# Expert 0's rows by one-hot products instead of a gather, three experts' lists from one-hot rows, and weight loads held back

## The chip, the cores and the metric

The kernel runs on one core of one Trainium2 chip. The metric is the device time of one execution in microseconds (us); smaller is better. Beside it stands a profile of one execution: what each engine did, when it waited and for whom. The engines are TensorE (PE, matrix products), VectorE (DVE), ScalarE (ACT), GpSimd (POOL) and SyncE (SP, which issues DMA transfers).

## What is computed

```
x   = attention(q, k, v)           # 2 x 8 heads, 768 positions, 64 wide; only where both hash to one bucket
x   = (silu(x @ w_in)) @ w_out     # 1536 tokens, 512 -> 2048 -> 512
do  = x @ w_skip > 0               # tokens that go on
e   = argmax(x[do] @ w_gate)       # one of 8 experts; gate = its softmax weight
y   = gate * (relu(x[do] @ w1[e]) @ w2[e])     # 512 -> 1024 -> 512
out = x;  out[do] = x[do] + y
```

## The kernel before

The work has three stages: attention, the MLP, and the experts. All is fp32; the large products are made of two halves each, a rounded high half (whi, xTh, gh) and the rest as low half (wlo, xTl, gl), three products for one. The high half is a copy on ScalarE, the low half a subtraction on VectorE.

**MLP.** The 1536 tokens go in three blocks of 512 (four tiles of 128 tokens each), the 16 pieces of the weights inside. When a block is done, its rows go to a DRAM buffer `x_d` and to the output, and for the first two blocks the gate logits are made on VectorE (`logit`, four per piece of the next block). Then `route` turns the logits of a block into places: which expert each token goes to, and its rank there, by small products with a triangular matrix. The tokens' numbers go to a list in DRAM, `id_d`, by an indirect DMA per tile (`tk` by `slot`), and the running lists of experts 0 and 1 are also made on chip: `oh` is a one-hot row per token, and `idx` and `idx1` are small products of it with the tokens' numbers.

**The bridge.** The third block is computed turned (features by tokens). It is turned back (`xt`), stored, and routed in the same way, expert 0 first, so that its rows can be gathered from `x_d` by an indirect DMA (`fetch_x(0)`) as soon as their list is there; then expert 1, the places of all tokens, and the gates (`gates`, `gp`, `gT`, `g_d`). Filler products (`em_busy`) stand between PE's steps.

**Experts.** `plan` is a list of steps, written out by hand, that sets the order: `("h", e, c, j)` is half a hidden block of expert e (12 products for a block, 6 in a step, `eh`), `t` turns it (`tr`, then hT0h/hT0l or hT1h/hT1l), `y` is the second product (`ey`), `x` turns the gathered rows of an expert (xTh/xTl), and after its last `y` an expert's result `eo` is scattered to the output. The weights of an expert are 8 pieces of 512 KB, 64 in all. Raw pieces land in 20 buffers (12 in `ring`, 8 in `more`; `fill` loads the next). `splitting` makes the two halves of a piece in one of 7 homes, and `ahead`, after most steps of the plan, splits as many further pieces as there are free homes. So in each engine's queue the halves of a piece stand up to seven pieces ahead of its use. Each engine works through its queue in order.

`fill(n, True)` loads n pieces, each behind a tiny memset on POOL, so that they start only when POOL has come to that place in its queue; `cnt["hold"]` stops all other loads.

## Time and profile before

| | |
|---|---|
| median of three runs | 622.31 us (621.67 to 625.53) |
| the profiled execution's own time | 622.04 us |
| its span, first to last instruction | 620.3 us |
| mean granted TensorE clock | 0.998 of full speed |
| busy: PE, DVE, ACT, POOL | 97%, 75%, 65%, 27% of the span |
| last MLP product ends, expert 0 begins (PE) | 499.13 us, 511.72 us |

Busy shares are means over three stages with different limits. A busy PE is not a PE at its peak. What a change in one stage is worth must be read from that stage: which wait ends last there.

### The profile page before, as it was taken

To read this page: it belongs to the slowest core of one execution; us is meant where nothing else is said; L and a number is where in the kernel's file an instruction comes from. 1 tells how busy PE (TensorE), PEld (TensorE's weight loads), DVE (VectorE), ACT (ScalarE), POOL (GpSimd) and SP (SyncE) were. 2 spreads that over 40 slices of the span, in tenths; PEclk is the share of its full clock that TensorE was granted. 3 is DMA by queue.
4 is the path that set the end of the run, shared out by engine and by line. 5 is a ranking of instruction groups with operands and counts; after the bars stand their busy time and mean duration, and the time that the engine had idled before them with its cause. 6 is when DMAs were issued, how large, how long until landed. Compare 5 with 4: busy or idle time off the path is not lost.

```text
span 620.3 us, 9579 instructions
## 1 busy us (share of the span) xinstructions
PE 604.2 (97%) x3263; PEld 463.3 (75%) x3263; DVE 465.7 (75%) x861; ACT 400.7 (65%) x671; POOL 167.3 (27%) x256
## 2 busy tenths in 40 slices
PE   8899999999999999999999999999999979999996
PEld 5767667676666757788888887788888857788885
DVE  6877777888787667799747775457885469899992
ACT  6988888888877985466554333443334456888881
POOL 5535637373653143000000000020000054534101
PEclk9999999999999999999999999999999999999999
DMA  4433542524324131666423000024232349999900
GB/s 134 144 113 93 174 124 58 157 66 137 79 66 122 46 115 52 214 216 229 143 89 121 1 1 1 1 47 164 97 103 101 118 150 257 395 408 408 391 20 28
DMA packets 30978, 83.47 MB, mean 135 GB/s; under 512 B 6032, under 2 KB 9810, under 8 KB 30798
## 3 DMA queue, kind: packets, MB, share of 16 engines
q1 hardware_dynamic: 28834, 79.06, 38.6%
q0 software_dynamic: 1936, 3.65, 1.7%
q8 instruction: 26, 0.43, 0.3%
q14 instruction: 26, 0.21, 0.1%
q10 hardware_dynamic: 156, 0.11, 0.1%
HBM read 67.66 MB, written 8.50 MB: 123 GB/s over the span
## 4 chain that ended last, share of the span: by engine, by line
PE 87%; DVE 4%; ACT 3%; DMA 2%; issue 2%; POOL 1%; SPq 0%; POOLq 0%; DVEq 0%; ACTq 0%
PE ph L605 20%; PE o L648 13%; PE S L385 11%; PE T L411 10%; PE pv L425 10%; PE o L639 7%; PE eh L1046 6%; PE ey L1068 6%; ACT P L399 1%; PE tr L1024 1%; PE pj L337 1%; DVE wlo L252 1%; PE bs L472 1%; DMA w<-in_mw_dram 1%; ACT K L317 1%
## 5 line engine op out<-in xcount | busy, mean ns | idle before, releaser
L252 DVE TENSOR_TENSOR wlo<-wraw,whi 128x1024 fp32r<-128x1024 f32 x100 | 119.6, 1222 | 5.8 <-ACT whi L249 4.9
L249 ACT CAST whi<-wraw 128x1024 fp32r<-128x1024 f32 x100 | 102.7, 1050 | 20.0 <-DVE wraw L223 13.1
L399 ACT ACTIVATE P<-S,bs 128x768 f32<-128x768 f32 x96 | 95.5, 994 | 27.1 <-DVE bs L397 25.3
L611 ACT ACTIVATE g<-ph 128x512 f32<-128x512 f32 x48 | 28.6, 597 | 119.8 <-PE ph L605 113.1
L395 DVE TENSOR_REDUCE mx<-S 128x1 f32<-128x768 f32 x96 | 91.1, 949 | 11.1 <-PE S L385 8.8
L385 PE MATMUL S<-K,Q 88*128 88x384 f32 (+1 forms) x384 | 92.3, 361 | 3.1 <-ACT P L399 3.0
L411 PEld LDWEIGHTS T<-ident,P 128*128 128x128 f32 x576 | 68.1, 141 | 30.8 <-ACT PT L414 22.1
L411 PE MATMUL T<-ident,P 128*128 128x128 f32 x576 | 88.7, 277 | 0.2 <-ACT PT L414 0.2
L613 DVE TENSOR_TENSOR gl<-g,gh 128x512 fp32r<-128x512 f32 x48 | 33.6, 701 | 68.9 <-ACT gh L612 68.9
L777 POOL DMA_INDIRECT id_d<-tk,slot x12 | 12.2, 1014 | 248.1 <-DVE pre L785 245.0
L425 PE MATMUL pv<-PT,v 128*64 128x384 f32 x384 | 72.3, 498 | 0.0
L385 PEld LDWEIGHTS S<-K,Q 88*128 88x128 f32 (+1 forms) x384 | 62.7, 191 | 11.7 <-ACT P L399 5.8
L416 DVE COPY PT<-T 128x384 f32<-128x384 f32 x85 | 47.0, 553 | 22.5 <-PE T L411 22.4
L414 ACT COPY PT<-T 128x384 f32<-128x384 f32 x107 | 50.5, 479 | 7.1 <-PE T L411 6.8
L605 PE MATMUL ph<-xhi,whi 128*128 128x512 f32 x192 | 52.9, 397 | 0.0
L605 PE MATMUL ph<-xhi,wlo 128*128 128x512 f32 x192 | 51.8, 392 | 0.7 <-DVE wlo L252 0.7
L605 PE MATMUL ph<-xlo,whi 128*128 128x512 f32 x192 | 51.9, 392 | 0.0
L325 POOL TENSOR_TENSOR K<-raw,K 64x192 fp32r<-64x192 f32 x56 | 31.6, 594 | 53.9 <-ACT K L317 28.9
L661 DVE CUSTOM_DVE_ANT_0 junk<-x,gwb 128x512 bf16<-128x512 f32 x72 | 45.4, 687 | 0.0
L330 POOL TENSOR_TENSOR Q<-raw,Q 64x192 fp32r<-64x192 f32 x64 | 36.1, 592 | 28.1 <-ACT Q L320 26.4
L605 PEld LDWEIGHTS ph<-xhi,wlo 128*128 128x128 f32 x192 | 36.0, 188 | 9.0 <-DVE wlo L252 1.2
L425 PEld LDWEIGHTS pv<-PT,v 128*64 128x64 f32 x384 | 23.4, 136 | 25.7 <-issue 25.6
(173 smaller groups left out, 1045.6 us busy)
## 6 DMA issues: line engine op xcount, KB each, us to landing
wraw<-in_w_dram SPq DMA_DIRECT2D x64, 512.0 KB
w<-in_mw_dram SPq DMA_DIRECT2D x32, 512.0 KB
v<-in_vt_dram SPq DMA_DIRECT2D x8, 384.0 KB
rb<-r_d SPq DMA_DIRECT2D x32, 96.0 KB
out_dram<-x SPq DMA_DIRECT2D x12, 256.0 KB
x_d<-x SPq DMA_DIRECT2D x11, 256.0 KB
raw<-in_kT_dram SPq DMA_DIRECT2D x7, 384.0 KB
raw<-in_qT_dram SPq DMA_DIRECT2D x7, 384.0 KB
```

What stands on the lines that cost most here:

```text
L249: nc.scalar.copy(hi[:, sl], t[:, sl])
L252: eng.tensor_tensor(lo[:, sl], t[:, sl], hi[:, sl].bitcast(F32), op=ALU.subtract)
L385: nc.tensor.matmul(ps[:, c, 0:HQ], q_[0:n, hd, q0:q0 + P], k_[0:n, hd, c * HQ:(c + 1) * HQ], start=first, stop=not first)
L395: nc.vector.tensor_reduce(mx[:, 0:1], ps[:, :, 0:HQ], axis=AX.XY, op=ALU.max, negate=True)
L399: nc.scalar.activation(pt.rearrange("p (a b) -> p a b", a=2), ps[:, :, 0:HQ], AF.Exp, bias=bs_[:, 0:1], scale=bs_[:, 1:2], accum_out=st_su ...
L411: nc.tensor.transpose(ps[:, j], pt[:, k * P:(k + 1) * P], ident)
L414: nc.scalar.copy(dst, ps)
L416: nc.vector.tensor_copy(dst, ps)
L425: nc.tensor.matmul(st_pv[u][hd * D:(hd + 1) * D], vts[i][:, k, hd], st_PT[u][:, hd, k], start=(k == 0), stop=(k == KT - 1))
L605: nc.tensor.matmul(p_[:, 0:c1 - c0], w[:, k * P:(k + 1) * P], x[:, k, t0 * P + c0:t0 * P + c1], start=(q == 0), stop=(q == len(ops3) - 1))
L648: nc.tensor.matmul(acc[t], g[:, (t - t0) * P:(t - t0 + 1) * P], w[:, DM:PIECE], start=(f == 0 and q == 0), stop=(f == NF - 1 and q == 2))
L661: nc.vector.tensor_tensor_reduce(junk, xts[t], pools["gwb_t"][:, c], op0=ALU.mult, op1=ALU.add, scale=1.0, scalar=0.0, accum_out=L[:, t, c ...
```

## The change

Expert 0's rows are no longer gathered before its first product. The rows in the first two blocks are gathered during the MLP's last pieces (`xg0`) and turned (`xT0p`); those in the third block are picked out by fp32 products of its tiles (`late`) with one-hot columns (`ohf`), four for each quarter of the features (`picked`), and the two are added (`summed`) and split (`parted`). The gather `fetch_x(0)` is still made, later, since the result needs the rows themselves. Lists on chip are made for three experts (`NL`), and the DRAM list is read for the other five. Logits of the first blocks come five per piece. In the bridge the logits are made before the tiles are turned, all turned tiles are copied by ScalarE, and there are 5 filler products instead of 37. The low halves of four split pieces, the third list, the places, the gates and their store, the list of the other experts and the largest count now stand between steps of the plan (`between`). Weight loads start behind the gathers of experts 1 and 2, behind that of expert 0, and behind the read of the list, and the last rows' stores to the output behind these; the gates are stored by ScalarE's queue. During expert 0's steps `ahead` is not called.

```diff
+++ after.py
     slot = cp.tile([P, NT], I32, name="slot")
     gat = cp.tile([P, NT], F32, name="gat")
-    list1 = cp.tile([P, 1], F32, name="list1")
+    lists = cp.tile([P, NL], F32, name="lists")
     eid = cp.tile([P, NE], I32, name="eid")
...
-    def gathered(ix, src, cols, tag):
-        xg = pools["e"].tile([P, cols], F32, tag=tag, name=tag, bufs=4)
+    def gathered(ix, src, cols, xg):
+        if isinstance(xg, str):
+            xg = pools["e"].tile([P, cols], F32, tag=xg, name=xg, bufs=4)
         nc.gpsimd.indirect_dma_start(
             out=xg, out_offset=None, in_=src, in_offset=bass.IndirectOffsetOnAxis(ap=ix, axis=0),
-            bounds_check=NTOK, oob_is_err=False)
+            bounds_check=src.shape[0] - 1, oob_is_err=False)
...
-        oh0 = onehot(0, pr0, st0)
-        yield
-        for j in range(n):
-            nc.tensor.matmul(idx, oh0[:, j], c_tok[:, t0 + j], start=False, stop=(last and j == n - 1))
-        if last:
-            with nc.allow_low_precision(reason="integers below 2048, exact"):
-                nc.vector.tensor_reduce(eid[:, 0:1], idx, axis=AX.X, op=ALU.add)
-            fetch_x(0)
...
+    def keyed(pr, st, n):
+        key = sm.tile([P, n], F32, tag="key", name="key")
+        nc.vector.scalar_tensor_tensor(key.unsqueeze(2), pr, 1.0, st, op0=ALU.add, op1=ALU.mult)
+        return key
+
+    def onehot(oh, key, n):
+        nc.vector.tensor_tensor(oh, c_iota.unsqueeze(1).to_broadcast([P, n, P]),
+                                key.unsqueeze(2).to_broadcast([P, n, P]), op=ALU.is_equal)
+
+    def places(e, pr, st, n):
+        key = keyed(pr, st, n)
+        oh = sm.tile([P, 5, P], BF16, tag=f"oh{e}", name="oh", bufs=1)
+        onehot(oh[:, 0:n], key, n)
+        return oh
+
+    def listed(dst, oh, t0, t1):
+
+        for j in range(t1 - t0):
+            nc.tensor.matmul(dst, oh[:, j], c_tok[:, t0 + j], start=(j == 0), stop=(j == t1 - t0 - 1))
+
+    def added(dst, ps, e):
         p1 = sm.tile([P, 1], F32, tag="p1", name="p1")
-        nc.vector.tensor_reduce(p1, idx1, axis=AX.X, op=ALU.add)
-        nc.vector.tensor_tensor(eid[:, 1:2] if last else list1, p1, list1, op=ALU.add)
-        if last:
-            fetch_x(1)
-        yield
-
-        sf = sm.tile([P, n], F32, tag="sf", name="sf")
+        nc.vector.tensor_reduce(p1, ps, axis=AX.X, op=ALU.add)
+        nc.vector.tensor_tensor(dst, p1, lists[:, e:e + 1], op=ALU.add)
...
+    def route(t0, t1, Lx, ps):
+
...
+        yield
+        ranks(pr, st, n, NE)
+        yield
+        sl = sm.tile([P, n, NE], F32, tag="sl", name="sl")
+        nc.vector.tensor_tensor(sl, pr, c_e0.unsqueeze(1).to_broadcast([P, n, NE]), op=ALU.add)
+        ohs = [places(e, pr[:, :, e:e + 1], st[:, :, e:e + 1], n) for e in range(NL)]
+        nc.vector.tensor_tensor(sl, sl, st, op=ALU.mult)
+        yield
+        for e in range(NL):
+            listed(ps[:, 464 + 16 * e:467 + 16 * e], ohs[e], t0, t1)
+        for e in range(NL):
+            added(lists[:, e:e + 1], ps[:, 464 + 16 * e:467 + 16 * e], e)
+        if t0:
+            eidp = sm.tile([P, 1], I32, name="eidp", bufs=1)
+            nc.vector.tensor_scalar(eidp, lists[:, 0:1], float(t1 * P), None, op0=ALU.min)
+            xg0 = gathered(eidp, x_d[0:t1 * P + 1], DM, pools["xo"].tile([P, DM], F32, tag="x", name="xg0", bufs=6))
+        slots(t0, t1, sl)
+        counts(t0, t1)
+        if t0:
+            yield
+            yield
+            yield
+            xtp = ps_tile("xtp", [P, KD, P], "O4")
+            for k in range(KD):
+                nc.tensor.transpose(xtp[:, k], xg0[:, k * P:(k + 1) * P], ident)
+            some.append(pools["xo"].tile([P, DM], F32, tag="x", name="xT0p", bufs=6))
+            nc.scalar.copy(some[0], xtp.rearrange("p k c -> p (k c)"))
...
+                for r in (TILES[-1][0] * P, NTOK):
+                    nc.sync.dma_start(x_d[r:r + 1].rearrange("o (p c) -> (o p) c", p=P), zx)
...
-                for j in range(4):
+                for j in range(5):
...
+        assert cnt["spl"] == NM + 3
+        sp = [splitting(NM + i, apart=True) for i in range(3, 7)]
...
+        ex = sm.tile([P, NT, NE], F32, name="gex", bufs=1)
+        nc.scalar.activation(ex[:, 0, 0:1], lists[:, 0:1], AF.Exp, scale=0.0)
...
-        xps = [ps_tile("xt", [P, KD, P], tag) for tag in ("O0", "O1", "H", "O2", "H")]
-        for k0 in (0, 2):
-            for t in range(t1 - t0):
-                for k in (k0, k0 + 1):
-                    nc.tensor.transpose(xps[4 if t == 0 and k0 else t][:, k], xt[k][:, t * P:(t + 1) * P], ident)
...
+        plc = sm.tile([32 * n, P], F32, name="plc", bufs=1)
+        nc.vector.tensor_copy(plc, plt[0:32 * n])
+
+        xps = [ps_tile("xt", [P, KD, P], tag) for tag in ("O0", "O1", "H", "O2")]
         late = []
...
-                (nc.vector.tensor_copy if t % 2 else nc.scalar.copy)(
-                    x[:, sl].rearrange("p (k c) -> p k c", c=P), xps[4 if k0 else t][:, k0:k1])
-                nc.sync.dma_start(x_d[(t0 + t) * P:(t0 + t + 1) * P, sl], x[:, sl])
+
+        def turned(t):
+            for k in range(KD):
+                nc.tensor.transpose(xps[t][:, k], xt[k][:, t * P:(t + 1) * P], ident)
+            x = ep.tile([P, DM], F32, tag="lx" if t < 2 else "eo", name="x")
+            nc.scalar.copy(x, xps[t].rearrange("p k c -> p (k c)"))
+            nc.sync.dma_start(x_d[(t0 + t) * P:(t0 + t + 1) * P], x)
             late.append(x)
...
-        sp = [splitting(NM + i, apart=True, eng=nc.vector) for i in range(3, 7)]
-        for g in sp:
-            next(g)
...
-        em_busy(5)
-        for j, _ in enumerate(route(t0, t1, pl, ps_tile("pr", [P, 512], "O3"), idx, ps_tile("pr0", [P, 512], "O0"))):
-            em_busy((5, 0, 4, 3, 0, 10)[j])
-            if j == 2:
-                fill(3, True)
-        next(gt, None)
+        turned(0)
+        nc.tensor.transpose(plx[:, P:P + 32 * n], plc, ident[0:32 * n, 0:32 * n])
...
+        turned(1)
+        em_busy(3)
+        ranks(pr0, st0, n, 1)
+        base(pr, t0, n, NE)
+        key = keyed(pr0, st0, n)
+        ohf = pools["xo"].tile([P, DM], F32, tag="x", name="ohf", bufs=6).rearrange("p (t c) -> p t c", c=P)
+        for c in range(0, n, 2):
+            onehot(ohf[:, c:c + 2], key[:, c:c + 2], 2)
+        turned(2)
+        turned(3)
+        xT0 = [ps_tile("xT0", [P, 2, P], tag) for tag in ("H", "O0")]
+
+        def picked(k):
+
+            for t in range(n):
+                nc.tensor.matmul(xT0[k // 2][:, k % 2], late[t][:, k * P:(k + 1) * P], ohf[:, t], start=(t == 0), stop=(t == n - 1))
...
+        def summed(j):
+            nc.vector.tensor_tensor(xs0[:, 2 * j:2 * j + 2], xT0[j], xs0[:, 2 * j:2 * j + 2], op=ALU.add)
+            nc.scalar.copy(xTs0[0][:, 2 * j:2 * j + 2], xs0[:, 2 * j:2 * j + 2])
+
+        def parted(j):
+            hi, lo, x = (x[:, 2 * j:2 * j + 2] for x in (*xTs0, xs0))
+            nc.vector.tensor_tensor(lo, x, hi.bitcast(F32), op=ALU.subtract)
...
+        nc.scalar.copy(ohb[:, 0:n], ohf)
+        next(sp[0])
+        choice(t0, t1, pl, mxl)
         nc.vector.tensor_copy(L[:, t0:t1], pl)
-        gp = ps_tile("gp", [P, 512], "O1")
-        nc.tensor.transpose(gp[0:NT, 0:P], gat, ident)
-        gT = sm.tile([NT, P], F32, name="gT", bufs=1)
-        nc.scalar.copy(gT, gp[0:NT, 0:P])
-        nc.sync.dma_start(g_d[0:NTOK].rearrange("(t p) c -> t (p c)", p=P), gT)
-        fill(3, True)
-        fetch_g(0)
...
-        def fetch_list():
-
-            nc.scalar.dma_start(eidr, id_d.rearrange("(e r) c -> e (r c)", e=NE)[2:NE, 0:P])
+        gt = gates(0, NT)
+        next(gt)
+        st = sel[:, t0:t1]
+        picked(0)
+        picked(1)
+        ranks(pr, st, n, NE)
+        summed(0)
+        next(sp[1])
...
+        ohs = [ohb] + [sm.tile([P, 5, P], BF16, tag=f"oh{e}", name="oh", bufs=1) for e in (1, 2)]
+        onehot(ohs[1][:, 0:n], keys[0], n)
+        picked(2)
+        picked(3)
+        parted(0)
+        onehot(ohs[2][:, 0:n], keys[1], n)
+        for e in (0, 1):
+            listed(ps[:, 464 + 16 * e:467 + 16 * e], ohs[e], t0, t1)
+        summed(1)
+        next(sp[2])
+        next(sp[3])
+        added(eid[:, 1:2], ps[:, 480:483], 1)
+        fetch_x(1)
+        added(eid[:, 0:1], ps[:, 464:467], 0)
+        parted(1)
+        next(sp[0], None)
...
-        xTs[0] = parts(xgs[0], "xT", 2)
-        next(sp[0], None)
-        next(sp[1], None)
-        next(sp[2], None)
-        next(sp[3], None)
-        nc.vector.tensor_copy(mxc, mxf)
+        xTs[0] = tuple(xTs0)
+
+        def third_list():
+
+            ps = psE.tile([P, KD, P], F32, tag="T", name="li", bufs=3)
+            listed(ps[:, 0, 0:3], ohs[2], t0, t1)
+            added(eid[:, 2:3], ps[:, 0, 0:3], 2)
+            fetch_x(2)
+            fill(3, True)
+            nc.vector.tensor_tensor(sl, sl, st, op=ALU.mult)
+            slots(t0, t1, sl)
+            fetch_x(0)
+            fill(3, True)
+            next(sp[1], None)
+            next(gt, None)
+
+        def gates_out():
+
+            gp = psE.tile([P, KD, P], F32, tag="T", name="gp", bufs=3)
+            nc.tensor.transpose(gp[0:NT, 0], gat, ident)
+            gT = sm.tile([NT, P], F32, name="gT", bufs=1)
+            nc.scalar.copy(gT, gp[0:NT, 0])
+            nc.scalar.dma_start(g_d[0:NTOK].rearrange("(t p) c -> t (p c)", p=P), gT)
+            fetch_g(0)
+            fetch_g(1)
+            nc.gpsimd.dma_start(eidr, id_d.rearrange("(e r) c -> e (r c)", e=NE)[NL:NE, 0:P])
+            fill(1, True)
+            for t, x in enumerate(late):
+                nc.sync.dma_start(out[(t0 + t) * P:(t0 + t + 1) * P], x)
+            cnt["hold"] = 0
+
+        def other_lists():
+
+            ps = psE.tile([P, KD, P], F32, tag="T", name="eT", bufs=3)
+            nc.tensor.transpose(ps[:, 0, 0:NE - NL], eidr, ident[0:NE - NL, 0:NE - NL])
+            nc.vector.tensor_copy(eid[:, NL:NE], ps[:, 0, 0:NE - NL])
+            fetch_x(3)
+            fetch_g(2)
+
+        def largest():
+
+            ps = psE.tile([P, KD, P], F32, tag="T", name="pc", bufs=3)
+            nc.tensor.matmul(ps[:, 0, 0:NE], c_one, pre[:, NT], start=True, stop=True)
+            nc.vector.tensor_reduce(mxc, ps[:, 0, 0:NE], axis=AX.X, op=ALU.max)
+
+        def one_ahead():
+
+            next(sp[3], None)
+            split(cnt["spl"])
+
+        between = {("h", 0, 0, 0): third_list, ("h", 0, 0, 1): lambda: next(sp[2], None), ("h", 0, 1, 0): gates_out,
+                   ("t", 0, 0): one_ahead, ("y", 1, 0): other_lists, ("h", 3, 0, 0): lambda: counts(t0, t1), ("y", 3, 0): largest}
...
-        for t, x in enumerate(late):
-            nc.sync.dma_start(out[(t0 + t) * P:(t0 + t + 1) * P], x)
-        fill(1, True)
-        cnt["hold"] = 0
-        fill()
...
-            if (what, e, *at) == ("y", 0, 0):
-                fetch_list()
-            if (what, e, *at) == ("h", 1, 0, 0):
-                ps = psE.tile([P, KD, P], F32, tag="T", name="eT", bufs=3)
-                nc.tensor.transpose(ps[:, 0, 0:NE - 2], eidr, ident[0:NE - 2, 0:NE - 2])
-                nc.vector.tensor_copy(eid[:, 2:NE], ps[:, 0, 0:NE - 2])
-                fetch_x(2)
-                fetch_g(2)
-                fetch_x(3)
-
-            if n + 1 == len(plan) or plan[n + 1][0] not in "tx":
+            between.get((what, e, *at), int)()
+            if (e or (what, *at) == ("t", 1)) and (n + 1 == len(plan) or plan[n + 1][0] not in "tx"):
                 ahead()
```

In VectorE's queue, from the low half of expert 1's rows to that of expert 2's (xTl 128x512 each; wlo is the low half of one weight piece, eid the cast of the other experts' list), there stood:

```order
L1018 TENSOR_TENSOR xTl<-tr,xTh 128x512
L1018 TENSOR_TENSOR hT1l<-tr,hT1h 128x512
L252 TENSOR_TENSOR wlo<-wraw,whi 128x1024
L1123 CAST eid<-eT 128x6
L252 TENSOR_TENSOR wlo<-wraw,whi 128x1024 x3
L1076 SCALAR_TENSOR_TENSOR eo<-ey,gg,xg 128x512
L1018 TENSOR_TENSOR hT0l<-tr,hT0h 128x512
L252 TENSOR_TENSOR wlo<-wraw,whi 128x1024 x4
L1018 TENSOR_TENSOR xTl<-tr,xTh 128x512
```

and now stands, with what is ahead of it since expert 0's first turned half (hT0l):

```order
L1060 TENSOR_TENSOR hT0l<-tr,hT0h 128x512
L253 TENSOR_TENSOR wlo<-wraw,whi 128x1024 x2
L1060 TENSOR_TENSOR xTl<-tr,xTh 128x512
L1060 TENSOR_TENSOR hT1l<-tr,hT1h 128x512
L253 TENSOR_TENSOR wlo<-wraw,whi 128x1024 x7
L1118 SCALAR_TENSOR_TENSOR eo<-ey,gg,xg 128x512
L1060 TENSOR_TENSOR hT0l<-tr,hT0h 128x512
L253 TENSOR_TENSOR wlo<-wraw,whi 128x1024 x4
L1162 CAST eid<-eT 128x5
L253 TENSOR_TENSOR wlo<-wraw,whi 128x1024
L1060 TENSOR_TENSOR xTl<-tr,xTh 128x512
```

Eight low halves stood between the two xTl, twelve do now, and the cast of the list has moved behind eleven of them.

In POOL's queue, from the last expert-list gathers of the bridge on (tk by slot is the scatter of token numbers, gg a gather of gates, the memset a weight load's gate), there stood:

```order
L669 DMA xg<-x_d,eid 128x512
L181 MEMSET wraw 1x1 x3
L669 DMA xg<-x_d,eid 128x512
L777 DMA id_d<-tk,slot 12288x1 x4
L181 MEMSET wraw 1x1 x3
L669 DMA gg<-g_d,eid 128x1 x2
L181 MEMSET wraw 1x1
L669 DMA xg<-x_d,eid 128x512
```

and now stand the gathers of experts 1 and 2, the scatters, the gather of expert 0, and the read of the list behind the gates:

```order
L671 DMA xg<-x_d,eid 128x512 x2
L182 MEMSET wraw 1x1 x3
L739 DMA id_d<-tk,slot 12288x1 x4
L671 DMA xg<-x_d,eid 128x512
L182 MEMSET wraw 1x1 x3
L671 DMA gg<-g_d,eid 128x1 x2
L1152 DMA eidr<-id_d 5x128
L182 MEMSET wraw 1x1
L1049 DMA out_dram<-eo,eid 1536x512
```

The read of the list (eidr), which ScalarE's queue issued, has moved onto POOL, ahead of the memset that lets the weight stream go.

On PE the transposition of the gates (gp) stood ahead of expert 0's first product:

```order
L987 MATMUL gp<-ident,gat 12x128
L1024 MATMUL tr<-ident,xg 128x128 x4
L1046 MATMUL eh<-whi,xTh 128x512
L1046 MATMUL eh<-wlo,xTh 128x512
L1046 MATMUL eh<-whi,xTh 128x512
```

and now stands inside expert 0, between its third block of six products and the turning of its first hidden block (hr):

```order
L1088 MATMUL eh<-whi,xTl 128x512 x2
L1146 MATMUL gp<-ident,gat 12x128
L1066 MATMUL tr<-ident,hr 128x128 x4
L1088 MATMUL eh<-whi,xTh 128x512
L1088 MATMUL eh<-wlo,xTh 128x512
```

The turning of the gathered rows (tr from xg) ahead of expert 0 is gone, and gp has moved behind eighteen of its products.

## Rows read from the trace of the kernel before

**Rows 1.** The page: busy time by engine, and the chain's shares.

```profile
PE 604.2 (97%) x3263; PEld 463.3 (75%) x3263; DVE 465.7 (75%) x861; ACT 400.7 (65%) x671; POOL 167.3 (27%) x256
...
PE 87%; DVE 4%; ACT 3%; DMA 2%; issue 2%; POOL 1%; SPq 0%; POOLq 0%; DVEq 0%; ACTq 0%
```

**Rows 2.** Stretches: from:to, length, busy us (instructions) by engine, clock, DMA share, GB/s.

```profile
499.13:511.72 12.59, 9.15 (x111) 6.76 (x109) 8.19 (x40) 8.01 (x14) 6.02 (x9) 1.00 0.54 162
511.72:520.00 8.28, 7.23 (x32) 5.58 (x32) 8.23 (x11) 5.78 (x8) 2.64 (x6) 1.00 0.86 172
520.00:532.70 12.70, 12.41 (x58) 9.82 (x59) 11.43 (x13) 9.10 (x11) 9.57 (x7) 1.00 0.96 366
...
543.40:555.90 12.50, 12.50 (x61) 10.24 (x61) 12.11 (x14) 10.53 (x14) 4.65 (x3) 1.00 1.03 406
```

**Rows 3.** The chain that ended last, from 490 us: start, us, what.

```profile
500.87 1.05 PE pl L946 x32
...
504.58 0.27 PE idx L749 x4
...
512.52 2.05 DVE wlo L252 x2
...
522.18 0.45 PE tr L1024 x4
...
526.72 2.79 PE ey L1068 x12
```

**Rows 4.** Timeline of PE: start, us, line, operation, out<-in, shapes, idle before.

```profile
502.30 0.33 PE L958 MATMUL pl<-ident,plc 128*128 128x128 f32 x1 [0.41 <-DVE plc L957]
...
510.76 0.28 PE L987 MATMUL gp<-ident,gat 128*12 128x128 f32 x1 [0.87 <-DVE gat L915]
...
520.05 0.73 PE L1068 MATMUL ey<-whi,hT0l 128*128 128x512 f32 x2 [1.10 <-DVE hT0l L1018]
...
537.68 0.63 PE L1046 MATMUL eh<-whi,xTl 128*128 128x512 f32 x2
...
542.34 0.60 PE L1024 MATMUL tr<-ident,xg 128*128 128x128 f32 x4
```

**Rows 5.** Timeline of POOL.

```profile
506.72 1.04 POOL L669 DMA_INDIRECT xg<-x_d,eid  x1 [5.47 <-DVE oh L742]
...
521.01 3.27 POOL L669 DMA_INDIRECT gg<-g_d,eid  x1 [0.30 <-issue]
```

**Rows 6.** Groups of DVE by shape: line, tile, count, busy, mean ns, idle before.

```profile
L661 DVE CUSTOM_DVE_ANT_0 junk<-x,gwb 128x512 bf16<-128x512 f32 x72 | 45.4, 687 | 0.0
L613 DVE TENSOR_TENSOR gl<-g,gh 128x512 fp32r<-128x512 f32 x48 | 33.6, 701 | 68.9 <-ACT gh L612 68.9
```

**Rows 7.** Timeline of DVE.

```profile
503.83 0.69 DVE L742 TENSOR_TENSOR oh<-ct,key 128x512 bf16<-128x512 f32 x1
...
512.44 4.62 DVE L252 TENSOR_TENSOR wlo<-wraw,whi 128x1024 fp32r<-128x1024 f32 x4
...
523.31 0.69 DVE L1018 TENSOR_TENSOR xTl<-tr,xTh 128x512 fp32r<-128x512 f32 x1
...
525.85 0.15 DVE L1123 CAST eid<-eT 128x6 int32<-128x6 f32 x1
...
536.66 0.68 DVE L1018 TENSOR_TENSOR xTl<-tr,xTh 128x512 fp32r<-128x512 f32 x1
```

**Rows 8.** Timelines of ACT and of SP.

```profile
501.30 1.28 ACT L911 ACT_TABLE_LOAD   x1
...
524.40 25.15 SPq L182 DMA_DIRECT2D wraw<-in_w_dram  x22
```

**Rows 9.** By tile: POOL's scatters (id_d), ns min/median/max; gathers' landing (xg).

```profile
L777 POOL DMA_INDIRECT id_d<-tk,slot x12: 969/973/1203, 408.0 to 513.3; - x12
...
DMA to landing us min/median/max: 3.6/7.1/8.2
```

More of the change, by code (lines that the diff above doesn't have):

```diff
@@ L678, in fetch_g, with base @@
         ggs[e] = gathered(eid[:, e:e + 1], g_d, 1, "gg")
[L681 to L705 removed]
+    def base(pr, t0, n, w):
+        nc.tensor.matmul(pr, c_one, pre[:, t0, 0:w].unsqueeze(1).to_broadcast([P, n, w]), start=True, stop=False)
@@ L706, in route, with ranks, choice @@
+    def ranks(pr, st, n, w):
+        for t in range(n - 1):
+            nc.tensor.matmul(pr[:, t + 1:n], c_one, st[:, t:t + 1].to_broadcast([P, n - 1 - t, w]), start=False, stop=False)
+        nc.tensor.matmul(pr, c_u, st, start=False, stop=True)
+    def choice(t0, t1, Lx, mx):
+        n = t1 - t0
+        cm = cmp_[:, t0:t1]
+        em = c_em.unsqueeze(1).to_broadcast([P, n, NE])
         nc.vector.tensor_scalar(cm, Lx[:, :, NE], 0.0, None, op0=ALU.is_gt)
         eq = sm.tile([P, n, NE], F32, tag="eq", name="eq")
-        em = c_em.unsqueeze(1).to_broadcast([P, n, NE])
@@ L728, in route @@
-        ch = choice()
-        next(ch)
-        if not last:
-            next(ch)
-            yield
-            ranks(pr, st, NE)
-            yield
-        sl = sm.tile([P, n, NE], F32, tag="sl", name="sl")
-        def onehot(e, pr, st):
-            key = sm.tile([P, n], F32, tag="key", name="key")
-            nc.vector.scalar_tensor_tensor(key.unsqueeze(2), pr, 1.0, st, op0=ALU.add, op1=ALU.mult)
-            oh = sm.tile([P, 5, P], BF16, tag=f"oh{e}", name="oh", bufs=1)
-            nc.vector.tensor_tensor(oh[:, 0:n], c_iota.unsqueeze(1).to_broadcast([P, n, P]),
-                                    key.unsqueeze(2).to_broadcast([P, n, P]), op=ALU.is_equal)
-            return oh
@@ L759, in route @@
-        oh1 = onehot(1, pr[:, :, 1:2], st[:, :, 1:2])
-        nc.vector.tensor_tensor(sl, sl, st, op=ALU.mult)
-        yield
-        idx1 = ps[:, 480:483]
-        for j in range(n):
-            nc.tensor.matmul(idx1, oh1[:, j], c_tok[:, t0 + j], start=(j == 0), stop=(j == n - 1))
-        p1 = sm.tile([P, 1], F32, tag="p1", name="p1")
-        nc.vector.tensor_reduce(p1, idx1, axis=AX.X, op=ALU.add)
-        nc.vector.tensor_tensor(eid[:, 1:2] if last else list1, p1, list1, op=ALU.add)
-        if last:
-            fetch_x(1)
@@ L840 @@
         nc.vector.memset(pre[:, 0], 0.0)
[L841 removed]
+        nc.vector.memset(lists, float(DUMMY))
         N = len(items)
[L844 removed]
+        routing = None
         for n in range(N + 1):
@@ new lines @@
+        base(pr, t0, n, NE)
+        key = keyed(pr0, st0, n)
[6 more added lines that the diff above has]
+        def picked(k):
+            for t in range(n):
+                nc.tensor.matmul(xT0[k // 2][:, k % 2], late[t][:, k * P:(k + 1) * P], ohf[:, t], start=(t == 0), stop=(t == n - 1))
@@ new lines @@
+        xTs0 = [ep.tile([P, KD, P], F32R, tag="xT" + c, name="xT" + c) for c in "hl"]
+        xs0 = some[0].rearrange("p (k c) -> p k c", c=P)
+        def summed(j):
[4 more added lines that the diff above has]
+            nc.vector.tensor_tensor(lo, x, hi.bitcast(F32), op=ALU.subtract)
```

105 lines of the change are left out of this document (37 added, 68 removed).

## Prediction

> **What bounds the kernel now.** I read the page first: TensorE (PE) is busy 97% of the span, and the chain that ended last is 87% PE [rows 1]. So an edit pays only where PE is not the last to finish. The table of stretches shows where that is [rows 2]: from 499.13 us (the last MLP product ends) to 511.72 us (expert 0's first product begins) PE is busy 9.15 of 12.59 us, partly with filler products; from 511.72 to 520 it is busy 7.23 of 8.28; from 543.4 on 12.50 of 12.50. The change lies in the first two stretches; the MLP before them and the experts after them run at PE's own pace.
>
> The chain says what fills the bridge [rows 3]: transposing the last tiles, their logits (pl, 1.05 us at 500.87), then many short VectorE (DVE) steps up to the gates, for which the transposition gp waits until 510.76 [rows 4]. Beside them runs expert 0's gather, issued at 506.72 [rows 5]. Right behind, the chain is DVE again: the low halves wlo from 512.52 [rows 3], and PE waits 1.10 us at 520.05 for hT0l [rows 4], which stands behind six wlo in DVE's queue. DVE is nearly as tight as PE here: in 520 to 532.7 it is busy 11.43 of 12.70 us, and later 12.11 of 12.50 [rows 2]. That decides the forecast.
>
> **The change, part by part.** All times are us on the profile's clock.
>
> MLP. Lists for three experts instead of two cost four more small products in each of two rounds (four: 0.27), and the rows of expert 0 that are found early are transposed once (four transpositions: 0.45) [rows 3]. This is on PE's path: 0.45 to 1.0, I take 0.7, so the MLP ends at 499.8. The fifth logit per step (0.69 each) runs on DVE, which waits 68.9 us in all before its 48 gl [rows 6]; I cost it at nothing, and without that cover it would be 0.7 for each of some 16 steps at most.
>
> Bridge. The logits now come first: pl ends at about 501.0, where it ended at 501.92 [rows 3]. After one tile's transposition its own (0.33 [rows 4]) gives the logits at 501.75, against 502.63. Max, choice, ranks and key take some 1.3 as before; the one-hot rows, two halves of what takes 0.69 now [rows 7], are there by 503.9. ScalarE (ACT) loads its table (1.28 [rows 8]), which used to come after its copies, and then copies four turned tiles at half a us each: the last is there at 504.45. PE starts the picks at 504.05.
>
> The picks are 16 fp32 products of 128 columns with a full 128x128 stationary block, which the trace does not have. From below: a transposition of that shape, 0.45 / 4 = 0.11. From above: pl, 16 products with 32 stationary columns in 1.05 [rows 3]; if four of them ran side by side, one costs 0.26. Both are fp32, but only pl multiplies, so I take 0.25, 4.0 in all (1.8 to 4.2). With 0.2 for ranks and 0.25 for two lists between, expert 0 starts at 508.5 instead of 511.72: 3.2 earlier, and no gather is waited for.
>
> Expert 0. New waits stand here. gp is now queued on PE behind the third block of six products (1.40 each, half of 2.79 [rows 3]) and waits for the gates on DVE. DVE, from 508.4 on: second sum of the picks, two lists and a low half (1.3), one wlo (1.15), the third list (0.4), the slots (0.8), another wlo (1.15), the gates (0.6): 513.8. PE would be there at 508.5 + 3 x 1.40 + 0.15 = 512.85, so gp waits 0.9, and behind it stands all the rest of expert 0. Then 0.25 + 0.45 + 1.40 + 2.79: PE turns expert 1's rows at 518.65, and ACT has xTh at 519.75. Before, xTl of expert 1 began at 523.31 [rows 7]. So far 3.55 is won; the old wait of 1.10 is gone with it.
>
> Expert 1, where it is lost. At that xTl DVE has split 8 pieces, where before it had split 12: four that ran in expert 0's time now come after it, because lists, slots and gates took their place. As the order shows, DVE must run seven wlo, eo, hT0l, four wlo, the cast of the list and one more wlo before xTl of expert 2. One wlo takes (4.62 - 1.22) / 3 = 1.13 from start to start in a packed row [rows 7], and up to 1.17 elsewhere; ACT has the first high half for them at 521.3. So 521.3 + 12 x 1.15 + 0.66 + 0.60 + 0.12 = 536.5 (the last three are busy times of 0.75, 0.68 and 0.15 less the same overlap of 0.1), and xTl ends at 537.2; now it ends at 536.66 + 0.68 = 537.34 [rows 7]. PE needs it for products that begin at 537.68 now [rows 4] and would begin at 537.25. Of 3.55 us, 0.4 is left.
>
> Then the gather of expert 3. Its list is cast on DVE behind eleven of those wlo, at 535.2, where the cast now is at 525.85 [rows 7]. POOL issues the gather at 535.6. Gathers land 3.6 to 8.2 after issue, median 7.1 [rows 9]; the shortest fits the first one, before the weights streamed, so I take 7.1: 542.7. PE wants the rows at 542.34 - 0.4 = 541.9 [rows 4] and waits 0.8 (0 to 1.9). Net 0.4 later than before. From there PE has no gaps [rows 2], so nothing more is won or lost. The last scatter and its wait are not touched.
>
> Weights. Pieces 15 to 17 start some 5 us later, the stream as early as now (524.40 [rows 8]), but with the four last stores in it. Piece 21, the first of it, is split some 13 us after it starts. I price the delay at nothing; the cover is that lead, and beyond it each us of delay is a us.
>
> Sum: the profiled execution is 622.04 (span 620.3 and 1.74 around it), 0.27 under the median of the three runs. 622.04 + 0.4 = **622.4**; the bounds of MLP (0.3 either way), picks (down to -0.5, since DVE's own steps bind then; up to +0.2) and gather (-0.8 to +1.1) make 620.8 to 624.0 of it.
>
> [...] POOL's 12 scatters take 0.97 to 1.20 each [rows 9], one small gather beside wlo took 3.27 [rows 5]. [...]
>
> **Rivals.**
> 1. PE sets the pace and DVE has room: expert 1 keeps the 3.55, and the time is 618.5. For it: PE shows no long wait after 520.05 now, and DVE is idle 1.27 us in 520 to 532.7 [rows 2]. Against it: the count of wlo between the two xTl, which nothing hides.
> 2. Slower: POOL gets late. In its queue the read of the other lists stands behind two gathers, four scatters, expert 0's second gather and two gathers of gates; at 1.3 from start to start it goes out at about 524, and PE wants it at 531. If each of those nine took 2.2 (midway between 1.0 and 3.27 [rows 5]), it goes out at 530.5 and lands some 4 later; eo of expert 0, which waits on DVE for its gate, holds hT0l behind it. That is 3.5 over the forecast: 625.9. It decides once they take over about 1.7 on average.
> 3. The change does not do what it says: a pick costs twice my price, expert 0 starts no earlier than now, and everything behind it 4.0 later than in the forecast: 626.4.
>
> **How the numbers follow.** Forecast 0.60, rival 1 0.20, rival 2 0.13, rival 3 0.07. The forecast's own range and rival 1 hold 0.80 from 618.5 to 624.0, but rival 1 has its bounds too, so the range goes on to rival 2: 618.5 to 625.9. One per cent, 6.2 us, is about what a measurement of this kernel tells from no change. The largest gain named is 3.5 and the largest loss 4.4, so within 1% gets 0.95; faster 0.02 and slower 0.03 are for two bounds that add.
>
> **What would show it.** Expert 0's first product about 9 us after the last MLP product (12.6 now); gp waiting about 1 us for gat; 12 wlo with hardly a gap between xTl of experts 1 and 2, and PE waiting 2 us or more in expert 1 for hr, hT0l or xTl; a short wait at the transposition of expert 3's rows. It is wrong if PE runs through experts 1 and 2 without waits (rival 1), if the transposition eT or eo waits for POOL's transfers (rival 2), or if the picks take 8 us (rival 3).

## The result and the profile after

The changed kernel takes 627.31 us (median of 13 runs) against 622.31 for the kernel before: a ratio of 1.0085, 95% interval 1.0068 to 1.0102. One of the 13 runs, at a mean granted clock of 0.75, took 749.99 us and is not in the ratio. So it is 5.0 us slower, where 622.4 was forecast, and 1.4 us above the top of the range, though within 1%. The profiled run of the changed kernel took 628.38 us, 1.07 above its median, with a span of 626.6; before it was 620.3, so the spans differ by 6.3.

The page of the changed kernel, busy time by engine and the chain's shares [rows 1]:

```profile
PE 608.5 (97%) x3274; PEld 466.1 (74%) x3274; DVE 468.4 (75%) x875; ACT 402.3 (64%) x674; POOL 168.5 (27%) x258
...
PE 84%; DMA 5%; issue 3%; ACT 3%; POOL 2%; DVE 1%; SPq 1%; POOLq 0%; DVEq 0%; ACTq 0%
```

PE has 4.3 us more of busy time, and DMA, 2% of the chain before, is 5% of it now: 3% of the span is some 19 us more of the chain in which a transfer is waited for. (That is not yet a loss: other steps left the chain.) The table of stretches says where. Columns as in [rows 2]:

```profile
501.36:509.20 7.84, 7.84 (x105) 7.28 (x105) 5.31 (x24) 7.10 (x12) 0.00 (x0) 1.00 0.37 137
509.20:520.00 10.80, 9.98 (x57) 7.71 (x54) 9.16 (x22) 5.19 (x8) 7.66 (x9) 1.00 0.47 158
520.00:532.70 12.70, 10.66 (x48) 7.95 (x46) 9.37 (x9) 12.67 (x16) 5.21 (x9) 1.00 0.87 257
532.70:543.40 10.70, 7.17 (x22) 5.40 (x23) 8.32 (x10) 3.06 (x5) 3.12 (x3) 0.68 1.03 414
549.39:562.00 12.61, 12.61 (x62) 10.38 (x62) 12.17 (x17) 10.71 (x15) 3.63 (x3) 1.00 1.03 403
```

The first row is the new bridge, from the end of the MLP to expert 0: 7.84 us, all of them busy, where it was 12.59 with 9.15 busy. That part did what it says. The loss is in the fourth row, 532.7 to 543.4: PE busy 7.17 of 10.70 us, at a mean granted clock of 0.68. From 549.39 to 562 PE has no gaps, as it had none from 543.4 to 555.9 before [rows 2]. PE's timeline of the changed kernel, the rows with a wait in front and the two that answer to [rows 4]:

```profile
514.66 0.28 PE L1146 MATMUL gp<-ident,gat 128*12 128x128 f32 x1 [0.82 <-DVE gat L916]
520.67 0.50 PE L1088 MATMUL eh<-whi,xTh 128*128 128x512 f32 x1 [0.24 <-ACT xTh L1059]
527.33 0.66 PE L1066 MATMUL tr<-ident,hr 128*128 128x128 f32 x4 [0.80 <-ACT hr L1093]
536.23 1.22 PE L1110 MATMUL ey<-whi,hT0l 128*128 128x512 f32 x2 [4.53 <-DVE hT0l L1060]
...
548.29 0.66 PE L1066 MATMUL tr<-ident,xg 128*128 128x128 f32 x4 [0.20 <-DMA xg<-x_d,eid]
```

PE stands 4.53 us at 536.23, for hT0l of expert 1. DVE's timeline shows why hT0l is late (it stands behind eo of expert 0):

```profile
522.08 8.08 DVE L253 TENSOR_TENSOR wlo<-wraw,whi 128x1024 fp32r<-128x1024 f32 x7
534.82 0.75 DVE L1118 SCALAR_TENSOR_TENSOR eo<-ey,gg,xg 128x512 f32<-128x512 f32 x1 [4.66 <-DMA out_dram<-x]
535.49 0.68 DVE L1060 TENSOR_TENSOR hT0l<-tr,hT0h 128x512 fp32r<-128x512 f32 x1
536.09 4.62 DVE L253 TENSOR_TENSOR wlo<-wraw,whi 128x1024 fp32r<-128x1024 f32 x4
540.64 0.15 DVE L1162 CAST eid<-eT 128x5 int32<-128x5 f32 x1
```

The wlo are done at 530.16, and eo then waits 4.66 us for "DMA out_dram<-x": the last stores. That is not data for eo. The third and fourth late tile (x in turned, tag "eo") share a ring of two buffers with eo, and eo, which takes the buffer of such a tile, starts at 534.82 behind the landing of a store; with buffers of their own for the late tiles (own_tiles, below) it waits for no store. The rest of the chain that ended last says how that reaches the end (start, us, what):

```profile
519.46 6.02 DMA id_d<-tk,slot
...
526.64 0.10 POOL wraw L182
...
527.14 0.45 SPq L1155
...
528.65 6.57 DMA out_dram<-x
535.22 0.02 issue
535.24 0.04 POOLq L1049
...
541.06 7.19 DMA xg<-x_d,eid
548.25 0.04 issue
548.29 1.09 PE tr L1066 x8
549.39 5.53 PE eh L1088 x24
```

The stores go out at 527.1 to 528.6, because they are queued on SP behind the weight piece whose memset (wraw, 526.64) stands on POOL behind the read of the experts' list, which itself waits for the last scatter of token numbers to land (525.47). Eo starts at 534.82, and the last of the four stores lands at 535.22. Eo, hT0l and four wlo follow, then the cast of the list at 540.64 (525.85 before [rows 7]), then the gather of expert 3, which lands at 548.25; PE wants its rows 0.2 us earlier. Before, the same stores went out at 515.9 to 518.5 (SP), and eo, 12 us behind the last of them, ran without a wait (DVE):

```profile
515.93 2.95 SPq L1094 DMA_DIRECT2D out_dram<-x  x4
...
530.66 0.75 DVE L1076 SCALAR_TENSOR_TENSOR eo<-ey,gg,xg 128x512 f32<-128x512 f32 x1
```

When they landed there, no view shows.

### The profile page after: what moved, and what is told of

Read it like the earlier page. It is cut to its first block, busy times and chain, and to the rows that moved or that the text cites. A ratio compares the mean times of both kernels' runs of the same rounds, so it can differ in the third digit from the quotient of the medians.

```text
span 626.6 us, 9608 instructions
## 1 busy us (share of the span) xinstructions
PE 608.5 (97%) x3274; PEld 466.1 (74%) x3274; DVE 468.4 (75%) x875; ACT 402.3 (64%) x674; POOL 168.5 (27%) x258
## 4 chain that ended last, share of the span: by engine, by line
PE 84%; DMA 5%; issue 3%; ACT 3%; POOL 2%; DVE 1%; SPq 1%; POOLq 0%; DVEq 0%; ACTq 0%
PE ph L606 20%; PE o L649 13%; PE S L386 11%; PE T L412 10%; PE pv L426 10%; PE o L640 7%; PE eh L1088 5%; PE ey L1110 4%; ACT P L400 1%; DMA xg<-x_d,eid 1%; PE pj L338 1%; PE tr L1066 1%; DMA out_dram<-x 1%; DMA id_d<-tk,slot 1%; PE bs L473 1%
## 5 line engine op out<-in xcount | busy, mean ns | idle before, releaser
L739 POOL DMA_INDIRECT id_d<-tk,slot x12 | 13.9, 1161 | 150.5 <-DVE pre L749 147.3
```

## The experiments

The ratio below is to the kernel before, run on the same chip; behind each median stand 6 to 13 runs. The last column is from the trace, in us: from the end of the last MLP product to the start of the transposition of expert 3's rows on PE's timeline. From there to the end of the span it is 77.9 and 78.0 us in the two kernels without the change and 78.2 to 78.4 in the changed kinds, so a gain ahead of it counts almost in full, except in own_tiles (79.9, the clock) and in the two kernels with "defer" (78.9 and 79.2, see there). The column leaves out how late the MLP itself ends, which varies by up to 2.5 us between the profiles of the changed kinds.

| kernel | median us | ratio, 95% | MLP's end to rows of expert 3 |
|---|---|---|---|
| before | 622.2 to 622.7 | 1 | 43.21 |
| changed | 627.31 | 1.0085 (1.0068 to 1.0102) | 46.93 |
| own_tiles | 627.97 | 1.0070 (1.0047 to 1.0093) | 45.44 |
| own_scatter_behind | 624.61 | 1.0027 (1.0009 to 1.0044) | 42.76 |
| stores_early | 623.94 | 1.0025 (1.0011 to 1.0039) | 42.92 |
| early_weights | 622.83 | 1.0008 (0.9990 to 1.0026) | 42.30 |
| early_defer | 620.91 | 0.9982 (0.9965 to 0.9999) | 40.23 |
| early_weights_defer | 621.06 | 0.9980 (0.9966 to 0.9994) | 39.45 |
| filler | 629.92 | 1.0111 (1.0091 to 1.0130) | 47.97 |
| before_stores_late | 628.89 | 1.0096 (1.0075 to 1.0117) | 49.33 |

### Buffers of their own for the late tiles

```diff
-            x = ep.tile([P, DM], F32, tag="lx" if t < 2 else "eo", name="x")
+            x = ep.tile([P, DM], F32, tag="lx", name="x", bufs=4)
```

> The changed kernel, with the one edit that all four late tiles of rows have buffers of their own, so that expert 0's output tile eo no longer takes the buffer of a late tile whose store is still under way. Theory (the wait of eo for the held stores is the cause): eo runs right behind the seventh low half wlo, at about 530.2 us instead of 534.82; PE waits under 0.4 us for hT0l instead of 4.53; the granted clock is 1.0 throughout; the list is cast 4.7 us earlier. Behind it PE still waits about 1.8 us at xTl of expert 2 (four wlo stand between) and about 1.4 us for the rows of expert 3, so the time falls from 627.3 to about 622.5 us (621.5 to 623.5). Rival, gates late: eo waits on its gate gg, whose gather was issued at 523.4, and the time falls by less than 2 us. Rival, MLP and lookahead: the 5 us come from the longer MLP and the wlo, the wait only covers them, and the time stays at 626 to 627.5.

Measured: 627.97 us, no gain. A miss. The wait that I named was gone, and yet the time was not. DVE of own_tiles, then POOL, then PE:

```profile
532.20 0.75 DVE L1118 SCALAR_TENSOR_TENSOR eo<-ey,gg,xg 128x512 f32<-128x512 f32 x1 [0.94 <-PE eh L1088]
...
538.00 0.16 DVE L1162 CAST eid<-eT 128x5 int32<-128x5 f32 x1
...
538.09 2.15 POOL L1049 DMA_INDIRECT out_dram<-eo,eid  x1 [10.13 <-DVE wlo L253]
540.54 1.98 POOL L671 DMA_INDIRECT xg<-x_d,eid  x1 [0.30 <-DVE hT1l L1060]
...
547.89 0.66 PE L1066 MATMUL tr<-ident,xg 128*128 128x128 f32 x4 [3.03 <-DMA xg<-x_d,eid]
```

Eo no longer waits for the stores. (It waits 0.94 for something else, its gate: that gather went out at 523.18 and landed 8.9 us later, 0.1 ahead of eo. In stores_early it took 8.04 and also ended 0.1 ahead of eo.) But eo's result is ready at 532.95, and its scatter goes out only at 538.09. The scatter writes the same output as the four stores (issued from 528.4 to 530.7; the last one took 6.57 us to land in the changed kernel), and I read the delay as a wait for their landing. (The row names a wlo as what released it, but that one had ended at 531.25. In stores_early, below, where the stores had gone out from 505.8 to 507.4, the same scatter went out 0.3 us after eo. In the changed kernel the chain puts POOL's queue at this scatter right behind a store's landing at 535.22, and the scatter starts at 536.05, 0.5 after eo.) POOL is idle for 10.13 us ahead of this scatter, 5.14 of them behind eo. Behind it in POOL's queue stands the gather of expert 3: its list is cast at 538.00, it goes out at 540.54, and PE waits 3.03 us for the rows. Here the granted clock was 0.87 in 543 to 556, and the 24 products behind those rows took 7.06 us instead of 5.53. So the held stores are waited for twice, by DVE for a buffer and by POOL for the output, and the two waits overlap. That it is the scatter that holds the gather, the next two runs show.

### The scatter behind the gather

```diff
+        behind = []
...
-                        scatter(eid[:, e:e + 1], o, out)
+                        if e:
+                            scatter(eid[:, e:e + 1], o, out)
+                        else:
+                            behind.append(o)
...
             fetch_x(3)
+            scatter(eid[:, 0:1], behind.pop(), out)
             fetch_g(2)
```

This is own_tiles with one more edit.

> The kernel with buffers of its own for the late tiles, and expert 0's scatter to out queued behind expert 3's gather on POOL instead of ahead of it. In the kernel with own buffers eo no longer waited for the stores (532.20 instead of 534.82, 1.1 of it a later start), but its scatter, which writes the same output, went out only at 538.09, when the stores had landed, took 2.15, and the gather of expert 3 behind it in POOL's queue went out at 540.54 although its list was cast at 538.00; PE waited 3.03 us for the rows. Theory (the held stores are waited for a second time, by the scatter that writes the same output): with the gather ahead, it goes out some 0.3 us after the cast, the wait of 3.03 falls to about 0.8, and the time falls from 628.0 to about 625.5 us (624.5 to 626.5). Rival, the gather's own landing (7.3 us among the weights) or the gate sets it: no fall beyond 0.7 us.

Measured: 624.61 us, 3.4 less than own_tiles. The gather now goes out right behind its list's cast (536.08):

```profile
536.51 1.79 POOL L671 DMA_INDIRECT xg<-x_d,eid  x1 [9.66 <-DVE eid L1166]
538.60 2.00 POOL L1049 DMA_INDIRECT out_dram<-eo,eid  x1 [0.30 <-issue]
```

No wait for the rows is left. This is the second path by itself, and it decides for the theory, in its wider form.

### The stores issued early

```diff
             fetch_x(2)
+            for t, x in enumerate(late):
+                nc.sync.dma_start(out[(t0 + t) * P:(t0 + t + 1) * P], x)
             fill(3, True)
...
-            for t, x in enumerate(late):
-                nc.sync.dma_start(out[(t0 + t) * P:(t0 + t + 1) * P], x)
             cnt["hold"] = 0
```

> The changed kernel, with the four last stores issued ahead of the first held weight pieces, right behind the gather of expert 2, instead of behind the read of the experts' list; buffers as in the changed kernel. Theory: the stores land by about 520, eo finds its buffer free, and the time is that of the kernel with buffers of its own, within 1 us (about 622.5). Rival, the hold is worth something: the stores delay the gathers of experts 1 and 2 or the scatters, and the time is more than 1 us above that of the kernel with own buffers. Rival, gates or MLP: 626 to 627.5.

Measured: 623.94 us. Both waits are gone at once, and of the loss of 5.0 us (0.85%) three tenths are left (0.25%). From the MLP's end to expert 3's rows it takes 42.92, 0.3 less than before. PE's timeline and DVE's of stores_early:

```profile
537.59 0.93 PE L1088 MATMUL eh<-whi,xTl 128*128 128x512 f32 x2 [1.57 <-DVE xTl L1060]
...
529.84 0.75 DVE L1118 SCALAR_TENSOR_TENSOR eo<-ey,gg,xg 128x512 f32<-128x512 f32 x1
...
535.64 0.16 DVE L1162 CAST eid<-eT 128x5 int32<-128x5 f32 x1
...
536.85 0.69 DVE L1060 TENSOR_TENSOR xTl<-tr,xTh 128x512 fp32r<-128x512 f32 x1
```

These are the times that the prediction drew: xTl of expert 2 at 536.85 (536.5 was forecast), the list's cast at 535.64 (535.2). But the MLP ended 1.2 us later here than forecast (500.96 instead of 499.8), so that counted from its end DVE was 0.8 us ahead of the forecast.

### The kernel before, with its stores late

```diff
+        fill(1, True)
+        fill(3)
         for t, x in enumerate(late):
             nc.sync.dma_start(out[(t0 + t) * P:(t0 + t + 1) * P], x)
-        fill(1, True)
         cnt["hold"] = 0
```

> The kernel before, with one edit: its four last stores are queued behind four more weight pieces, so that as in the changed kernel seven pieces stand ahead of them. Theory: they go out at about 527.4 and land at about 535, eo of expert 0 waits some 4 us where it ran at 530.66, hT0l comes some 4 us later, PE (which needs it at 533.5) waits about 2.5 us and later about 1 us more for xTl; the time rises by 2.5 to 4.5 us, to about 626. Rivals (gates, MLP, lookahead): no rise beyond 1 us, since nothing else of the change is in it.

Measured: 628.89 us, 6.3 more than before and more than the 2.5 to 4.5 expected. Nothing else of the change is in this kernel, and it has the same wait. DVE, then PE:

```profile
537.68 0.75 DVE L1076 SCALAR_TENSOR_TENSOR eo<-ey,gg,xg 128x512 f32<-128x512 f32 x1 [5.37 <-DMA out_dram<-x]
...
539.09 0.88 PE L1068 MATMUL ey<-whi,hT0l 128*128 128x512 f32 x2 [3.84 <-DVE hT0l L1018]
```

Eo waited 5.37 us (some 4 expected; the store that it waits for took 8.51 us to land), PE's wait was 3.84 instead of 2.5, and the granted clock fell to 0.83 in 533 to 543, which I had not counted. So late stores alone cost what the whole change lost and more.

### The clock held up through the wait

```diff
                     for q, (x, w, k) in enumerate(ORD(*hT[e, 2 * jj // KD], *ws[jj])):
+                        if (e, jj, q) == (1, 0, 4):
+                            bz = psE.tile([P, KD, P], F32, tag="T", name="fz", bufs=3)
+                            for _ in range(36):
+                                nc.tensor.matmul(bz[:, 0:2], c_u, cb[:, 0:256].rearrange("p (k c) -> p k c", c=P), start=True, stop=True)
```

> The changed kernel, with 36 filler products (bf16, 256 columns, about 4.5 us) on PE just ahead of the two products that wait 4.53 us for hT0l; DVE, the stores and the gathers are untouched. If the time lost behind the wait is the lower clock (0.68 in 532.7 to 543.4), the clock stays at 1.0 and the time falls by 2 to 3 us, to about 624.8. If the late list and its gather set the pace there (the rows of expert 3 land at 548.25 whatever PE does, and PE waits only 0.20 us for them), the clock stays at 1.0, the wait for those rows grows from 0.2 to about 3 us, and the time stays within 0.7 us of 627.3. The second is what I expect.

Measured: 629.92 us, 2.6 above the changed kernel, where I had expected at most 0.7 of change. The part that the run was for is clear. Stretches of filler:

```profile
533.00:543.00 10.00, 8.22 (x55) 6.13 (x52) 6.71 (x8) 4.08 (x6) 2.14 (x2) 1.00 1.04 412
543.00:556.00 13.00, 10.56 (x49) 8.48 (x50) 10.77 (x13) 8.23 (x11) 9.48 (x7) 1.00 1.03 404
```

The clock stays at 1.00, and nothing is won: PE now waits 1.55 us for xTl of expert 2, where it had no such wait, and 1.40 for the rows of expert 3 instead of 0.20, together about the 3 us expected. In the changed kernel the slow products lie in a time in which the late gather sets the pace anyway, so the low clock in 532.7 to 543.4 has no part in the 5 us that shows here. In this trace the stores landed in 7.62 us and the gather in 7.81, against 6.57 and 7.19, which is 1.7 more on the chain; that the fillers made them slower is not shown, and the rise of 2.6 stays open (in the profile, the column rose by 1.04 and the MLP ended 1.04 later).

### What is left: the lookahead on DVE

This is stores_early with one more edit: three times in expert 1 no further pieces are split.

```diff
+            if (what, e, *at) in (("h", 1, 1, 0), ("h", 1, 1, 1), ("y", 1, 0)):
+                continue
             if (e or (what, *at) == ("t", 1)) and (n + 1 == len(plan) or plan[n + 1][0] not in "tx"):
```

> The kernel with the last stores issued early (623.94 us), and the lookahead splits after the steps h(1,1,0), h(1,1,1) and y(1,0) left to later steps, so that two low halves wlo instead of five stand between hT0l of expert 1 and xTl of expert 2 on DVE. In stores_early PE waited 1.57 us for that xTl, and eight products behind it took 3.49 us (0.44 each, with the granted clock at 0.83 in 533 to 543). Theory (what is left of the loss is that lookahead, with the clock behind it, and the longer MLP): both go, some 2.5 to 3 us, to about 621.2 us (620.3 to 622.3). Rival: the three low halves come later and hold eo of expert 1 or xTl of expert 3 instead, or the rows of expert 3 are late: 623 to 625.

Measured: 620.91 us, as expected, and faster than the kernel before by 0.2% (interval 0.01 to 0.35%). The wait for xTl is gone, and the clock stays at 1.00 throughout. So the prediction's account of the lookahead was right as well: twelve wlo between the two xTl cost PE 1.57 us, and moving three of them frees it. Of the 2.7 us won up to expert 3's rows, some 0.6 are lost again behind them: from there to the hidden products behind expert 4's rows it takes 14.17 us, where early_weights, below, takes 13.53. The postponed splits come then, and PE waits 0.15 and 0.3 us for DVE.

### The weights' hold

This too is stores_early with one more edit.

```diff
-            fill(3, True)
+            fill(6)
             nc.vector.tensor_tensor(sl, sl, st, op=ALU.mult)
             slots(t0, t1, sl)
             fetch_x(0)
-            fill(3, True)
```

> The kernel with the last stores issued early, and with the six weight pieces that were held behind the gathers of experts 1 and 2 and behind the gather of expert 0 issued at once, right behind the stores. If the hold of the weights is worth nothing (my price in the prediction), the time stays within 0.7 us of 623.9. Rival, the gathers and scatters land later among 3 MB of weights: the rows of expert 1, wanted at 519.4 and issued at 510.5, come late, and the time rises by 1 to 4 us.

Measured: 622.83 us, 1.1 less than stores_early; the two intervals overlap (0.9990 to 1.0026 and 1.0011 to 1.0039). The rival is out: PE waits for expert 1's rows no more than it did, and the list is cast as early after the MLP (34.5 us, against 34.7); only the read of the list goes out 0.75 us later, which holds nobody. Holding the weights buys nothing here and may cost up to 1 us; against my bound of 0.7 that is a near miss.

> Last stores early, the six held weight pieces early, and the three lookahead splits of expert 1 left to later steps, in one kernel. Stores early alone took 623.94 us, with the splits moved 620.91, with the weights early 622.83. If the two edits act in different places (the weights ahead of 530 us, the splits behind it), they add: 619.8 us (619.0 to 620.8), faster than the kernel before (622.7). Rival, both only move PE to the next wait, that for the rows of expert 3 (0.92 us in early_weights, 0.18 in early_defer): 620.5 to 621.5.

Measured, with both edits: 621.06 us (0.9980, 0.9966 to 0.9994). They do not add, and the rival was right. Expert 3's rows are turned 0.8 us sooner after the MLP than in early_defer, but behind that PE waits 0.3 us for the next xTl, and at the hidden products behind expert 4's rows, at 556.8 us, 0.5 of the lead is left (53.96 us after the first logit product of the last tiles, against 54.47), which the medians don't show. The two are the fastest versions, and not to be told apart.

### The longer MLP

```diff
-                for j in range(5):
+                for j in range(4):
                     if todo:
```

> The kernel with the last stores issued early, and four logits per MLP step instead of five. From the second g of the MLP to the first logit product of the last tiles it is 258.2 to 258.3 us in the four profiles of the changed kind, and 257.7 to 257.9 in the two of the kernel before, in which 1.75 us of transpositions lie between; so the MLP itself is 2.1 us longer. If the fifth logit slows the products (0.93 us for four of them against 0.92 in one stretch), the distance falls to about 257.4. If not, and lists, early rows and the first wait for wlo make it, it stays at 258.2, within 0.15.

```diff
-        for e in range(NL):
+        for e in range(2):
             listed(ps[:, 464 + 16 * e:467 + 16 * e], ohs[e], t0, t1)
```

> The kernel with the last stores issued early; the lists of the earlier tiles are kept for two experts only, so the third expert's list lacks its rows of the first eight tiles (that part of the computation is left out). From the second g of the MLP to the first logit product of the last tiles it is 258.2 us with three lists. If the third list's eight products and its DVE steps make a good part of the 2.1 us by which the MLP is longer, the distance falls by 0.4 to 0.8; if only its products count, by 0.2; if it is the pace of the products or the early rows, by under 0.15.

The second edit is the same in the two lines that make the one-hot rows and add the lists. Both are stores_early with one more edit. One time of each is 625.34 and 625.55 us; what counts is the trace. ACT's 48 g mark the MLP's steps. (The expectations leave out the first: their second g is the third.) From the fourth to the last it is 241.06 us in the kernel before, 242.40 in the changed one, 242.41 with four logits, and 242.19 with two lists. So the fifth logit costs PE nothing, and the third list 0.2. With four logits, however, the whole distance grew from 258.2 to 259.62: the early rows of expert 0 came later, their transposition slid behind the last product, and PE waited before the logits of the last tiles, the second row here, with the transposition above it:

```profile
500.97 0.60 PE L786 MATMUL xtp<-ident,xg 128*128 128x128 f32 x4
502.78 1.36 PE L945 MATMUL pl<-xt,gwc 128*32 128x128 f32 x32 [1.21 <-issue]
```

So the fifth logit earns its place. With two lists the distance was 258.55, because the MLP's first wait for wlo was 1.50 us there; that wait lies between 0.56 and 1.50 in all profiles.

## Why the prediction was wrong, point by point

**The step that failed.** "Weights ... with the four last stores in it ... I price the delay at nothing; the cover is that lead." The lead I named was that of the weight pieces, 13 us ahead of their use. For the stores I asked nobody who waits for them. Two do: eo, which takes a buffer of a late tile, and expert 0's scatter, which writes the same output and has the gather of expert 3 behind it. Before, eo ran 12 us after the last store had gone out; the change moved the stores by 10 to 11 us, so that the last goes out 1.6 us ahead of the time at which eo could have run (530.2). The price: stores_early against the changed kernel, 4.0 us on the trace (46.93 against 42.92), 3.4 in the medians. One line of the code says the first of the two paths, tag "eo" on the late tiles, and it is in the kernel before too.

**The MLP, mis-sized.** I took 0.7 (0.45 to 1.0); it is 2.0 us longer. The transposition of the early rows is 0.44 as priced, the third list 0.2 (in each of two rounds, 12 products in 0.30 instead of eight in 0.20; I had counted 0.27 for every four), the first wait for wlo 0.96 instead of 0.73. Of the other 1.1 us most lies in steps that take 5.52 instead of 5.47 us in long stretches, with no wait in front of any product. The fifth logit is not its cause, nor the third list. What is, stays open.

**The bridge: right.** Sixteen picks took 3.77 us, 0.235 each (0.25 forecast), expert 0 began 7.84 us after the MLP (8.7, so 0.9 sooner than forecast), and gp waited 0.82 (0.9). The chain's two pieces:

```profile
505.30 1.89 PE xT L994 x16
...
507.28 1.88 PE xT L994 x16
```

Each pick is two records here. Rival 3, picks at twice the price, is out.

**Expert 1 and the lookahead: right, as soon as the stores are out of the way.** "Of 3.55 us, 0.4 is left" and a net 0.4 later at the end: stores_early has 42.92 us from the MLP to expert 3's rows where the kernel before has 43.21, and my steps gave 542.7 less 499.8, 42.9. Its median, 623.94, is my 622.4 and 1.5 for the MLP's missing 1.3. That the two 42.9 meet so closely is partly luck: DVE reached xTl of expert 2 0.8 us sooner after the MLP than I had it, and behind it the clock fell to 0.83 (last section), where eight products took 3.49 us instead of 2.13, which no term of mine has. At full clock, in early_weights, it is 42.30.

**The gather of expert 3: right in kind.** It was forecast to be issued at 535.6 and to hold PE 0.8 us. In early_weights it went out at 535.38, and PE waited 0.92. In stores_early it went out at 536.07, and PE, at the lower clock, came no sooner than the rows.

**Rival 2** named the right waiter, "eo of expert 0 ... holds hT0l behind it", and nearly the right price, but the wrong thing waited for. (Its sum is off, too: nine transfers at 2.2 instead of 1.3 from start to start put the read at 532.1, not 530.5, and the rival at 627.5.) POOL's four scatters took 0.97 to 1.40 us, its gathers up to 2, and the read of the list went out at 526.09, against 524 in the forecast and 530.5 in the rival; what it waited for was the last scatter's landing (525.47, 0.62 ahead of it), not POOL: as with the scatter of eo, the chain goes from the landing of a write to the transfer that uses the same tensor. Of the two rows that the prediction sets side by side, the scatters' [rows 9] and the small gather's [rows 5], the trace stays with the scatters': of the three scatters that ran beside wlo, two took 0.97 and 0.99 us, as the fourth did with DVE idle (0.97), and one 0.4 more; the two small gathers beside wlo took 1.01 and 1.95. What made the one of the kernel before slower, no view shows. Rival 1, PE without waits, is what early_defer comes near to.

## What to carry to other kernels

When a store or load is moved later, list who waits for its end, not only for its data: whoever takes its buffer next (here eo, 4.66 us in the changed kernel), the later writes to the same tensor (here expert 0's scatter, which went out 5.14 us behind eo in own_tiles), and all that is queued behind those on their engines (here the gather of expert 3, 2.54 us behind the start of its list's cast there). Look for the buffer in the pool's tag: here a shared tag made eo wait for the store of a tile that it has nothing to do with, and in own_tiles, without it, that wait was gone. And take both paths away before you call a wait unimportant: with one of two overlapping waits removed the time here did not move (627.31 and 627.97), with both it fell by 3.4.
